# A weight unit is loaded between the first two attention chunks and converted earlier

## The chip, the cores and the metric

The kernel runs on one core of a Trainium2 chip. The time is the device time of one execution in microseconds (us). Engines: PE multiplies matrices, ACT and DVE work element by element, POOL does a few scalings, and the transfers of the part that matters here are issued by SP. Each engine works through its own queue of instructions in order, so an instruction that waits holds everything queued behind it on that engine.

## The reference

```python
scores = scale * np.matmul(q, k.transpose(0, 1, 3, 2))          # 4 batches, 8 heads, 576 positions, 64 wide
Dmat = np.where(rel >= 0, gamma ** rel, 0.0)                    # rel = row - column, one gamma per head
x = np.matmul(scores * Dmat, v)                                 # -> 2304 tokens x 512
h = x @ w_in;  g = np.where(h > 0, h, np.exp(np.minimum(h, 0)) - 1);  x = g @ w_out      # 512 -> 2048 -> 512
h = np.maximum(x @ w_in2, 0);  out = (h * h) @ w_out2
```

The four weight matrices come as 64-bit floats, q, k and v as well as the result are 32-bit.

## The kernel before

**Attention.** The decay mask is a product of a factor of the row and a factor of the column, so q and k are scaled by such factors and what is left is a causal mask. Tokens are taken in five blocks and each block in chunks of at most 128 positions. Block 0 is chunks 0 to 3 of batch 0; block 1 begins with the last 64 positions of batch 0 (chunk 4), then chunks 5 to 8 of batch 1, of which chunk 8 again has 64. A chunk has three pieces (`attn_pieces`). `transposes`: PE transposes the scaled q and k (L304) and ACT copies them out (L309). `scores`: PE multiplies them (L317), DVE masks the two halves (L320, tile P or spare). `values`: PE multiplies the state of the earlier chunks (L332, tile st) and the masked scores (L336) into ps_o, ACT and DVE split the result in a high and a low part (L161, L162, tile x), PE makes the chunk's own sum (L346, ps_u) and DVE adds it to the state (L352, or L354 where the state starts). q and k of chunks 0 to 3 are scaled by POOL, of the others by DVE (L278).

**Weights of layer 1.** A unit is 128 rows or columns of w_in or w_out, 512 KB as it lies in memory. `load_raw` (L198, L203) fetches it into a tile raw, `to_f32` turns the 64-bit floats into 32-bit ones (ACT L215 and L216; DVE L217, L218, L219, L222; tile f), `split_w` splits them (ACT L161, DVE L162; tile w). Units are taken in the order of use: unit 0 and 1 are w_in 0 and 1, unit 2 is w_out 0, then w_in 2, w_out 1, w_in 3 and so on. `w1_to(n)` converts up to n units; in it `w1_run` issues loads ahead (five units while `NURSERY` has places), then a split, then a conversion.

**Feed-forward of layer 1.** For a block and a w_in unit, `up` makes h with 12 matmuls (L174, L175, L176: high by high, high by low, low by high), ACT and DVE make g of it (L378, L379, L380; L382, L383; L161, L162), and `down`, two steps later, makes 12 matmuls into acc. h has two buffers, and the third `up` can start only when the first h has been read for the last time, by L383.

**What sets the order.** The source is recorded in program order, and a scheduler then places each engine's instructions by its own estimate of times. Loads marked `keep_in_program_order` stay as written; `tc.issue_after(i)` holds what is recorded inside it behind instruction i in the schedule. The head of the kernel is written by hand: the loads, then the pieces of chunks 0 to 3 in the order of `pieces`, with `EARLY` giving the units that are to be converted after each. 14 multiplications with zeros (`idle`, L171) are put between the last chunks. Later chunks are spread over the first steps of the feed-forward by `SPREAD`.

Layer 2 follows with a scheme of seven products in place of eight; the change does not touch it.

Of the kernel before, what the change touches and what calls it, by code (L numbers as in the profile page):

```python
# [127 lines left out]
def tile_kernel(ctx: ExitStack, tc, q, k, v, w_in1, w_out1, w_in2, w_out2, cst, out):  # L128
# [35 lines left out]
    def last_of(engine):  # L164
        return next(i for i in reversed(nc.cur_bb.bb.instructions) if i.engine == engine)

    def idle(n, ps, start=False):


        for _ in range(n):  # L170
            nc.tensor.matmul(ps, zero, ident.bitcast(BF16), start=start, stop=True, skip_group_check=True)  # L171
# [10 lines left out]
    def raw_place():  # L182


        n = at["raw"]
        if n >= NURSED:
            return raw_p.tile([P, DM, 2], I32, tag="raw", name="raw")
        if len(nursery) == n:
            tag, k = NURSERY[sum(n >= sum(m for _, m in NURSERY[:i + 1]) for i in range(len(NURSERY)))]
            t = wp.tile([P, k, DM, 2], I32, tag=tag, name="raw")  # L190
            nursery.extend(t[:, i] for i in range(k))
        return nursery[n]

    def load_raw(layer, which, f):
        w = ((w_in1, w_out1), (w_in2, w_out2))[layer][which].bitcast(I32)
        t = raw_place() if layer == 0 else raw_p.tile([P, DM, 2], I32, tag="raw", name="raw")
        if which == 0:
            i = nc.sync.dma_start(  # L198
                out=t.rearrange("p (k f) t -> p k (f t)", k=KC),
                in_=w[:, 2 * f * P:2 * (f + 1) * P].rearrange("(k p) f -> p k f", p=P),  # L200
            )
        else:
            i = nc.sync.dma_start(out=t.rearrange("p c t -> p (c t)"), in_=w[f * P:(f + 1) * P, :])  # L203
        if layer == 0:
            tc.keep_in_program_order(i)
        raws[layer, which, f] = t
# [47 lines left out]
    def load_chunk(ch):  # L254
        b, s, n = ch
        ts = []
        if ch in aside:

            t = wp.tile([P, 6, DM], F32, tag=f"w{9 - aside.index(ch)}", name="spare")
            spare[ch] = [t[:, i] for i in range(6)]  # L260
        for i, (src, nm) in enumerate(((q, "q"), (k, "k"), (v, "v"))):
            if ch in aside:
                t = spare[ch][i].rearrange("s (h d) -> s h d", h=H)
            else:
                t = n_p.tile([P, H, D], F32, tag=nm, name=nm)
            tc.keep_in_program_order(
                nc.sync.dma_start(out=t[:n], in_=src[b, :, s:s + n, :].rearrange("h s d -> s h d"))
            )
            ts.append(t)
        nat[ch] = ts  # L270

    def scale_chunk(ch):
        n = ch[2]
        qn, kn, _ = nat[ch]

        eng = nc.gpsimd if ch in blocks[0] else nc.vector
        for t, c in zip((qn, kn), scale_cols(ch[1])):
            eng.tensor_tensor(  # L278
                out=t[:n], in0=t[:n], in1=cs[:n, c:c + H].unsqueeze(2).to_broadcast([n, H, D]), op=ALU.mult
            )  # L280
# [439 lines left out]
    w1 = [(0, *u) for u in units]  # L720
# [12 lines left out]
    def load_next(late=False):  # L733
        if at["load"] < len(chunks) and (late or chunks[at["load"]][1] < 2 or chunks[at["load"] - 1][1] >= 2):
            load_chunk(chunks[at["load"]][0])
            at["load"] += 1

    def scale_next():
        if at["scale"] < at["load"]:
            scale_chunk(chunks[at["scale"]][0])  # L740
            at["scale"] += 1
# [15 lines left out]
    def step(name, limit, todo_, work):  # L757
        if at[name] < min(limit, len(todo_)):
            work(todo_[at[name]])
            at[name] += 1  # L760

    def w1_to(n):


        if at["split"] < min(int(n), len(w1)):
            with tc.issue_after(last_of(mybir.EngineType.Activation)):
                w1_run(n)

    def w1_run(n):
        while at["split"] < min(int(n), len(w1)):  # L770
            while at["raw"] < min(at["f32"] + (AHEAD_NURSED if at["raw"] < NURSED else AHEAD), len(w1)):
                step("raw", 99, w1, lambda u: load_raw(*u))
            step("split", at["f32"], w1, split_w)
            step("f32", at["raw"], w1, to_f32)
# [1 line left out]

    new_x(0)
    first = [attn_pieces(ch, 0) for ch in blocks[0]]
    load_next()
    load_next()  # L780
    for u in w1[:2]:
        load_raw(*u)
        at["raw"] += 1
    load_next()
# [3 lines left out]
    pieces = ((0, 0), (1, 0), (0, 1), (1, 1), (0, 2), (2, 0), (1, 2), (3, 0), (2, 1), (3, 1), (2, 2), (3, 2))  # L788
    for (c, piece), n in zip(pieces, EARLY):
        first[c][piece]()  # L790
        if (c, piece) == (3, 1):
            scored = last_of(mybir.EngineType.PE)
        if (c, piece) == (2, 2):
            rest = ps_h.tile([P, 512], F32, tag="h", name="rest")
            with tc.issue_after(scored):
                idle(14, rest[:, :256], True)
        w1_to(n)
        if piece == 0 and c < 2:
            scale_next()
        if (c, piece) in ((0, 2), (2, 0)):  # L800
            load_next()
    scale_next()
    at["next"] = len(first)
    pend = []
    seq = [(0, 0), (0, 1), (1, 0), (1, 1), (0, 2), (1, 2)] + [(f, c) for f in range(2, HF - 2) for c in range(NCH)]
# [130 lines left out]
```

## Time and profile before

| | us |
|---|---|
| median of 3 runs | 884.81 (883.24 to 886.2) |
| profiled execution | 884.94 |
| its span, first to last instruction | 883.0 |
| PE busy | 857.5 (97%) |
| DVE busy | 685.4 (78%) |
| ACT busy | 490.0 (55%) |
| granted PE clock, mean | 0.999 of full speed |

The profiled execution is 0.13 us above the median, and 1.94 us of it lie outside of the span. Busy times overlap; what PE does not fill of the span is 25.5 us. The profile names an idle time by what ended it: `[0.78 <-DVE P L320]` is 0.78 us of waiting that the DVE instruction of line 320, writing P, ended. Instructions of one engine overlap a little at their ends, so the distance between two starts is less than the duration in the row.

### The profile page before, as it was taken

The page shows a single profiled execution, that of the slowest core. Times are in us where ns is not written, and L with a number is a line of the kernel's source. Part 1 is how long each engine was busy: PE and PEld are TensorE (multiplying, and loading weights), DVE is VectorE, ACT ScalarE, POOL GpSimd, SP SyncE. Part 2 cuts the span into 40 slices and gives each one's busy share as a digit, 9 for nine tenths or more (in the row PEclk, how much of TensorE's full clock was granted, in tenths as well). Part 3 has the DMA queues.
Part 4 walks back from the last instruction along what each step waited for, and adds up shares of the span by engine and source line. Part 5 has one row for each costly group of instructions (what it writes and reads, how often), then busy time and mean ns, then how long its engine had stood idle before and what let it go on. Part 6 is the DMA issues. An engine that isn't in the chain of part 4 may idle for free.

```text
span 883.0 us, 15049 instructions
## 1 busy us (share of the span) xinstructions
PE 857.5 (97%) x5671; PEld 769.9 (87%) x5671; DVE 685.4 (78%) x1391; ACT 490.0 (55%) x961; POOL 9.6 (1%) x13
## 2 busy tenths in 40 slices
PE   7898999999999999999999999999999899999998
PEld 5686888888888888888888899999999889999997
DVE  4998978885668777766779866889883869899984
ACT  4764878664365565655757744556553434444441
POOL 4000000000000000000000000000000000000000
PEclk9999999999999999999999999999999999999999
DMA  9944306473539647434362053599979993444330
GB/s 222 289 105 159 120 16 176 144 202 96 131 88 248 151 149 215 132 120 155 128 229 74 24 161 122 181 321 340 337 239 362 402 336 126 162 143 145 121 131 36
DMA packets 157608, 155.33 MB, mean 176 GB/s; under 512 B 62816, under 2 KB 121312, under 8 KB 157536
## 3 DMA queue, kind: packets, MB, share of 16 engines
q1 hardware_dynamic: 150208, 139.69, 51.7%
q10 hardware_dynamic: 7328, 14.68, 4.5%
q8 instruction: 44, 0.72, 0.3%
q14 instruction: 28, 0.23, 0.1%
HBM read 98.77 MB, written 55.57 MB: 175 GB/s over the span
## 4 chain that ended last, share of the span: by engine, by line
PE 77%; DVE 10%; DMA 7%; ACT 2%; issue 2%; ACTq 1%; SPq 1%; POOL 0%; DVEq 0%
PE m L691 18%; PE A L505 8%; PE acc L174 7%; PE acc L175 7%; PE acc L176 7%; PE h L174 7%; PE h L176 6%; PE h L175 6%; PE D L505 4%; PE B L505 2%; DMA g2s<-go 2%; PE ps_o L336 1%; PE ps_s L317 1%; DVE go L532 1%; PE ps_t L304 1%
## 5 line engine op out<-in xcount | busy, mean ns | idle before, releaser
L691 PE MATMUL m<-wo,S 128*128 128x256 f32 x1512 | 183.4, 283 | 2.8 <-ACT S L161 2.4
L691 PEld LDWEIGHTS m<-wo,S 128*128 128x128 f32 x1512 | 182.0, 192 | 4.1 <-ACT S L161 3.3
L161 ACT CAST S<-g 128x512 fp32r<-128x512 f32 (+1 forms) x144 | 74.8, 565 | 96.1 <-DVE g L672 46.9
L174 PE MATMUL h<-x,w 128*128 128x512 f32 (+1 forms) x320 | 119.3, 374 | 4.6 <-DVE t L383 3.6
L175 PE MATMUL acc<-g,w 128*128 128x512 f32 (+1 forms) x320 | 118.6, 372 | 0.3 <-DVE g L162 0.3
L176 PE MATMUL h<-x,w 128*128 128x512 f32 (+1 forms) x320 | 118.2, 369 | 0.0
L175 PE MATMUL h<-x,w 128*128 128x512 f32 (+1 forms) x320 | 117.9, 369 | 0.2 <-DVE x L162 0.2
L176 PE MATMUL acc<-g,w 128*128 128x512 f32 (+1 forms) x320 | 117.5, 370 | 0.0
L505 PE MATMUL A<-T,pair 128*128 128x384 f32 x576 | 113.8, 336 | 2.8 <-DVE go L532 1.7
L174 PE MATMUL acc<-g,w 128*128 128x512 f32 (+1 forms) x320 | 110.9, 375 | 1.0 <-ACT w L161 0.8
L505 PEld LDWEIGHTS A<-T,pair 128*128 128x128 f32 x576 | 100.5, 188 | 5.4 <-DVE go L532 3.6
L162 DVE TENSOR_TENSOR S<-g,S 128x512 fp32r<-128x512 f32 (+1 forms) x144 | 85.5, 619 | 20.9 <-ACT S L161 19.3
L378 ACT ACTIVATE t<-h 128x512 f32<-128x512 f32 (+1 forms) x80 | 44.3, 554 | 80.7 <-PE h L176 76.7
L382 DVE SCALAR_TENSOR_TENSOR t<-e,t 128x512 f32<-128x512 f32 (+1 forms) x80 | 50.6, 633 | 45.4 <-ACT t L380 45.0
L174 PEld LDWEIGHTS h<-x,w 128*128 128x128 f32 x320 | 60.0, 188 | 16.7 <-DVE t L383 4.0
L161 ACT CAST g<-t 128x512 fp32r<-128x512 f32 (+1 forms) x80 | 46.1, 578 | 46.6 <-DVE t L383 46.2
L174 PEld LDWEIGHTS acc<-g,w 128*128 128x128 f32 x320 | 59.4, 188 | 12.0 <-ACT w L161 1.0
L175 PEld LDWEIGHTS acc<-g,w 128*128 128x128 f32 x320 | 60.3, 188 | 10.6 <-DVE g L162 0.5
L176 PEld LDWEIGHTS h<-x,w 128*128 128x128 f32 x320 | 60.2, 188 | 10.5 <-DVE w L162 0.2
L175 PEld LDWEIGHTS h<-x,w 128*128 128x128 f32 x320 | 60.2, 188 | 10.3 <-DVE x L162 0.5
L176 PEld LDWEIGHTS acc<-g,w 128*128 128x128 f32 x320 | 60.2, 188 | 10.2
L505 PE MATMUL D<-T,pair 128*128 128x384 f32 x288 | 58.1, 335 | 0.6 <-DVE T L162 0.6
(93 smaller groups left out, 1283.2 us busy)
## 6 DMA issues: line engine op xcount, KB each, us to landing
g2s<-go SPq DMA_DIRECT2D x48, 384.0 KB, 4.9
g<-g2s SPq DMA_DIRECT2D x36, 512.0 KB, 4.0
raw<-in_moe_w_in_dram SPq DMA_DIRECT2D x32, 512.0 KB, 5.8
raw<-in_moe_w_out_dram SPq DMA_DIRECT2D x32, 512.0 KB, 4.6
wo2s<-wo SPq DMA_DIRECT2D x56, 256.0 KB, 4.3
wo<-wo2s ACTq DMA_DIRECT2D x9, 1536.0 KB, 15.5
w2s<-f SPq DMA_DIRECT2D x32, 256.0 KB, 2.3
f<-w2s SPq DMA_DIRECT2D x32, 256.0 KB, 4.3
```

Source lines behind the costliest of these rows:

```text
L161: nc.scalar.copy(pair_hi, src)
L162: eng.tensor_tensor(out=pair_lo, in0=src, in1=pair_hi.bitcast(F32), op=ALU.subtract)
L174: nc.tensor.matmul(ps, l_hi, r_hi, start=first, stop=False)
L175: nc.tensor.matmul(ps, l_hi, r_lo, start=False, stop=False)
L176: nc.tensor.matmul(ps, l_lo, r_hi, start=False, stop=last)
L304: nc.tensor.transpose(ps[:, p, :n], t[:n, 2 * p:2 * p + 2, :].rearrange("s h d -> s (h d)"), ident[:n, :n])
L317: nc.tensor.matmul(ps[e][:n, p, :n], kT[r, p, :n], qT[r, p, :n], start=True, stop=True)
L336: nc.tensor.matmul(ps[e * D:(e + 1) * D, p, :n], vn[:n, 2 * p + e, :], live[e][:n, p, :n], start=not s, stop=True, skip_group_check=True,)
L378: nc.scalar.activation(t, h, AF.Relu, scale=-1.0)
L382: nc.vector.scalar_tensor_tensor(out=t, in0=e, scalar=1.0, in1=t, op0=ALU.add, op1=ALU.mult)
L505: ins = nc.tensor.matmul(ps, w[:, l, o:o + P], t[:, r, j], start=first and i + j == 0, stop=i + j == 3, skip_group_check=True)
L691: ins = nc.tensor.matmul(m(u, k), l[:, x], w[:, y], start=first and k in (1, 6, 4, 5), stop=j == HF - 1 and i == 2, skip_group_check=True,)
```

## The change

Three edits, all in the head of the kernel. The load of unit 0 is issued between the loads of chunk 0 and chunk 1; unit 1 stays between chunk 1 and chunk 2. The conversion of unit 0 is recorded after the transposes of chunk 0 and its split after the scores of chunk 0, each behind the last ACT instruction so far. The scaling of chunk 4 is held behind the state sums of chunk 2. Since unit 0 is then split before `w1_to(1)` is called, that call does nothing, and the four further loads that it used to issue come with the next call, after the loads of chunk 4.

```diff
     new_x(0)
     first = [attn_pieces(ch, 0) for ch in blocks[0]]
-    load_next()
-    load_next()
     for u in w1[:2]:
+        load_next()
         load_raw(*u)
         at["raw"] += 1
     load_next()
@@
         first[c][piece]()
+        if (c, piece) == (2, 2):
+            masked = last_of(mybir.EngineType.DVE)
         if (c, piece) == (3, 1):
             scored = last_of(mybir.EngineType.PE)
...
+        if piece < 2 and c == 0:
+            with tc.issue_after(last_of(mybir.EngineType.Activation)):
+                step(*(("split", 1, w1, split_w) if piece else ("f32", 1, w1, to_f32)))
         w1_to(n)
         if piece == 0 and c < 2:
             scale_next()
         if (c, piece) in ((0, 2), (2, 0)):
             load_next()
-    scale_next()
+    with tc.issue_after(masked):
+        scale_next()
```

The order of instructions changes with it on PE, DVE, ACT and SP up to about the sixth `up`; from there on it is the same but for a few neighbours that change places late in the kernel.

On DVE, at the very start, this stood before (P_184 and P_186 are the masked scores of chunk 0, f and raw tiles of the weight conversion, st the state):

```order
L320 TENSOR_TENSOR P_184<-ps_s,cs 128x512
L320 TENSOR_TENSOR P_186<-ps_s,cs 128x512
L354 COPY st<-ps_u 64x4x64 x2
L217 TENSOR_SCALAR f<-f 128x512
L162 TENSOR_TENSOR x<-ps_o,x 128x4x128
L218 TENSOR_SCALAR f<-f 128x512
L320 TENSOR_TENSOR spare<-ps_s,cs 128x512
L217 TENSOR_SCALAR f<-f 128x512
```

and this stands there now (P_191 and P_193 are the masks, w_195 the split weights):

```order
L217 TENSOR_SCALAR f<-f 128x512
L218 TENSOR_SCALAR f<-f 128x512
L320 TENSOR_TENSOR P_191<-ps_s,cs 128x512
L320 TENSOR_TENSOR P_193<-ps_s,cs 128x512
L219 SCALAR_TENSOR_TENSOR f<-raw,f 128x512
L222 ISA f<-raw,f 128x1024
L162 TENSOR_TENSOR x<-ps_o,x 128x4x128
L354 COPY st<-ps_u 64x4x64 x2
L162 TENSOR_TENSOR w_195<-f,w_195 128x512
L320 TENSOR_TENSOR spare<-ps_s,cs 128x512 x2
```

Two instructions of unit 0's conversion went ahead of the masks of chunk 0, and all of unit 0 ahead of the masks of chunk 1; unit 1's, of which the first stood between those masks, went behind them.

On PE, around the scores of chunk 2, this stood before (spare holds q, k, their transposes and masks of chunks 1 to 3; the first row is a transpose of chunk 2):

```order
L304 MATMUL ps_t<-cs,spare 128x128 x4
L336 MATMUL ps_o<-spare 64x128 x7
L304 MATMUL ps_t<-cs,spare 128x128 x4
L317 MATMUL ps_s<-spare 128x128 x8
L304 MATMUL ps_t<-cs,spare 128x128 x8
L332 MATMUL ps_o<-spare,st 128x128 x4
```

and this stands there now:

```order
L336 MATMUL ps_o<-spare 64x128 x8
L304 MATMUL ps_t<-cs,spare 128x128 x8
L317 MATMUL ps_s<-spare 128x128 x8
L304 MATMUL ps_t<-cs,spare 128x128 x4
L332 MATMUL ps_o<-spare,st 128x128 x4
```

The scores of chunk 2 (L317) stood behind the two transposes of chunk 2 alone; now the transpose of chunk 3's q stands between them.

On PE, in front of the third `up` (its weights are w_328; P_510 is a mask of chunk 4, and q and k of chunk 5), this stood before:

```order
L336 MATMUL ps_o<-P_510,v 64x64
L304 MATMUL ps_t<-cs,q 128x128 x4
L174 MATMUL h<-x,w_328 128x512
L175 MATMUL h<-x,w_328 128x512
L176 MATMUL h<-x,w_328 128x512
```

and this stands there now:

```order
L336 MATMUL ps_o<-P_510,v 64x64
L304 MATMUL ps_t<-cs,q 128x128 x4
L304 MATMUL ps_t<-cs,k 128x128 x4
L317 MATMUL ps_s<-qT,kT 128x128 x8
L174 MATMUL h<-x,w_328 128x512
```

The other transpose and the scores of chunk 5 went ahead of the third `up`. On DVE the instruction that frees a buffer of h for this `up` is the first L383. These rows led up to it before:

```order
L217 TENSOR_SCALAR f<-f 128x512
L320 TENSOR_TENSOR P_508<-ps_s,cs 64x4x64
L320 TENSOR_TENSOR P_510<-ps_s,cs 64x4x64
L278 TENSOR_TENSOR k<-k,cs 128x512
L222 ISA f<-raw,f 128x1024
L162 TENSOR_TENSOR w_328<-f,w_328 128x512
L218 TENSOR_SCALAR f<-f 128x512
L382 SCALAR_TENSOR_TENSOR t<-e,t 128x512
L162 TENSOR_TENSOR w_328<-f,w_328 128x512
L219 SCALAR_TENSOR_TENSOR f<-raw,f 128x512
L383 TENSOR_TENSOR t<-h,t 128x512
```

and these do now:

```order
L217 TENSOR_SCALAR f<-f 128x512
L222 ISA f<-raw,f 128x1024
L218 TENSOR_SCALAR f<-f 128x512
L217 TENSOR_SCALAR f<-f 128x512
L219 SCALAR_TENSOR_TENSOR f<-raw,f 128x512
L218 TENSOR_SCALAR f<-f 128x512
L382 SCALAR_TENSOR_TENSOR t<-e,t 128x512
L162 TENSOR_TENSOR w_328<-f,w_328 128x512
L222 ISA f<-raw,f 128x1024
L162 TENSOR_TENSOR x<-ps_o,x 128x4x64
L219 SCALAR_TENSOR_TENSOR f<-raw,f 128x512
L383 TENSOR_TENSOR t<-h,t 128x512
```

Between the state sums of chunk 3 (the last L352 before these rows) and the first L383 there were 13 DVE instructions; now there are 20, among them one more unit's conversion.

## Rows read from the trace of the kernel before

**Rows 1.** Busy time by stretch of the span; a stretch's length stands before the comma.
```profile
0.00:9.50 9.50, 6.79 (x31) 3.59 (x32) 0.48 (x1) 2.46 (x3) 3.54 (x8) 1.00 0.99 188
9.50:25.00 15.50, 11.91 (x138) 9.45 (x140) 13.27 (x22) 9.18 (x16) 6.08 (x5) 1.00 1.11 270
25.00:44.00 19.00, 16.25 (x179) 13.62 (x179) 17.65 (x35) 12.90 (x25) 0.00 (x0) 1.00 1.09 278
44.00:67.00 23.00, 23.00 (x142) 18.83 (x143) 22.86 (x43) 15.38 (x28) 0.00 (x0) 1.00 0.45 105
67.00:92.00 25.00, 22.30 (x231) 17.73 (x230) 19.65 (x37) 12.25 (x24) 0.00 (x0) 1.00 0.42 138
92.00:883.00 791.00, 777.20 (x4956) 706.68 (x4954) 611.54 (x1255) 437.79 (x868) 0.00 (x0) 1.00 0.55 175
```

**Rows 2.** PE in order of time: start, duration, what; idle before it.
```profile
12.67 1.16 PE L317 MATMUL ps_s<-spare 64*128 64x128 f32 x16
...
19.35 1.16 PE L317 MATMUL ps_s<-spare 64*128 64x128 f32 x16 [0.68 <-ACT spare L309]
21.18 0.65 PE L304 MATMUL ps_t<-cs,spare 128*128 128x128 f32 x4 [0.67 <-POOL spare L278]
...
30.70 1.13 PE L332 MATMUL ps_o<-spare,st 128*128 128x128 f32 x8 [1.40 <-DVE st L352]
...
43.90 0.47 PE L174 MATMUL h<-x,w 128*128 128x512 f32 x1 [1.13 <-DVE t L383]
...
46.75 0.60 PE L304 MATMUL ps_t<-cs,k 128*128 128x128 f32 x4
47.10 1.17 PE L174 MATMUL acc<-g,w 128*128 128x512 f32 x4
...
67.56 1.16 PE L317 MATMUL ps_s<-qT,kT 64*128 64x128 f32 x16
69.50 1.16 PE L332 MATMUL ps_o<-qT,st 128*128 128x128 f32 x8 [0.78 <-DVE P L320]
```

**Rows 3.** Busy time of one microsecond; the last number is GB/s.
```profile
11.00:12.00 1.00, 1.00 (x18) 0.83 (x17) 0.00 (x0) 0.59 (x1) 0.00 (x0) 1.00 1.10 349
```

**Rows 4.** ACT in order of time, and its group of L378.
```profile
12.10 0.67 ACT L215 ACTIVATE raw<-raw 128x512 int32<-128x512 uint32 x1 [0.23 <-DMA raw<-in_moe_w_in_dram]
...
38.28 0.60 ACT L378 ACTIVATE t<-h 128x512 f32<-128x512 f32 x1 [0.73 <-PE h L176]
...
L378 ACT ACTIVATE t<-h 128x512 f32<-128x512 f32 (+1 forms) x80 | 44.3, 554 | 80.7 <-PE h L176 76.7
```

**Rows 5.** POOL in order of time.
```profile
8.29 1.04 POOL L278 TENSOR_TENSOR spare<-spare,cs 128x512 f32<-128x512 f32 x1 [1.34 <-DMA spare<-in_q_dram]
9.50 1.04 POOL L278 TENSOR_TENSOR spare<-spare,cs 128x512 f32<-128x512 f32 x1 [0.16 <-DMA spare<-in_k_dram]
...
19.79 2.79 POOL L278 TENSOR_TENSOR spare<-spare,cs 128x512 f32<-128x512 f32 x2 [2.54 <-DMA spare<-in_q_dram]
```

**Rows 6.** DVE in order of time.
```profile
9.53 1.29 DVE L320 TENSOR_TENSOR P<-ps_s,cs 128x512 f32<-128x512 f32 x2 [8.13 <-PE ps_s L317]
...
21.60 1.52 DVE L162 TENSOR_TENSOR w<-f,w 128x512 fp32r<-128x512 f32 x1
...
24.24 0.68 DVE L162 TENSOR_TENSOR w<-f,w 128x512 fp32r<-128x512 f32 x1
...
35.32 0.85 DVE L352 TENSOR_TENSOR st<-ps_u,st 64x256 f32<-64x256 f32 x2
...
43.08 0.68 DVE L383 TENSOR_TENSOR t<-h,t 128x512 f32<-128x512 f32 x1
43.68 0.41 DVE L217 TENSOR_SCALAR f<-f 128x512 f32<-128x512 f32 x1
44.01 0.41 DVE L162 TENSOR_TENSOR x<-ps_o,x 128x256 fp32r<-128x256 f32 x1
...
68.75 1.29 DVE L320 TENSOR_TENSOR P<-ps_s,cs 128x512 f32<-128x512 f32 x2
```

## The prediction

> **What bounds the kernel now.** Read busy time by stretch first [rows 1]: PE fills 777.20 of the last 791 us and every one of the 23 us from 44 to 67. What it leaves is 2.71 us (9.50 less 6.79) up to 9.5, 3.59 up to 25, 2.75 up to 44, none up to 67, 2.70 up to 92 and 13.80 after. From 92 on the changed kernel has the same order on every engine but for a few neighbours, so I take those 13.80 us as kept: the change can give or take only in the first 92 us, where 11.75 us are idle on PE, and the first 2.71 of them lie ahead of everything that it moves. Then read who is full in the head: DVE works 13.27 of 15.50 us from 9.5 to 25, 17.65 of 19.00 up to 44 and 22.86 of 23.00 up to 67. So until about 44 DVE sets the pace, from 44 to 67 PE and DVE are both full, and from 67 to 92 they wait for each other. Last read PE's waits in order of time: 1.40 us for state sums at 30.70, 1.13 us for L383 in front of the third up at 43.90, 0.78 us for a mask at 69.50 [rows 2]. A gain must show there: the same PE work reached earlier.
>
> **The transfers.** Nothing is added: the bytes are the same. Unit 0 takes the place of chunk 1's q. Chunk 1's q and k were there just before 8.29 and 9.50, where POOL starts on them [rows 5]; 1.2 us lie between them, so the queue began on q at about 7.05. Unit 0, 0.524 MB at 349 GB/s [rows 3], takes 1.5 us: it lands at about 8.55, not shortly before 12.10, where ACT waited for it [rows 4]. Chunk 1 comes 1.5 us later (q 9.75, k 10.95). From unit 1 on the sum of bytes ahead is as before; chunk 4 now precedes units 2 to 5, which come some 1.7 us later and are not waited for, since unit 2's conversion stands behind the masks of chunk 2.
>
> **The head, step by step.** ACT's L215 and L216 end 1.3 us after 8.55 (0.67 each [rows 4]), at 9.9. L217 and L218 take 0.33 each (43.68 to 44.01 [rows 6]), so the masks of chunk 0, now queued behind them, run from 10.6 to 11.9. They ran from 9.53 to 10.82 [rows 6]: 1.1 us later. Chunk 1's k leaves POOL at 12.05 (1.04 each [rows 5]), its transposes stand behind the masked products of chunk 0 on PE (some 1.5 us from 11.9) and its scores start at about 14.6, not 12.67 [rows 2]: 1.9 later. DVE's two early L217 and L218 are thus paid for by the masks behind them.
>
> The next gate takes that delay up: chunk 2's scores, which started at 19.35, now stand behind the transposes of chunk 3's q, and these waited for POOL until 21.18 [rows 2, 5]. With 0.6 us for the transposes the scores start at about 21.75, 2.4 us later than before, whatever happened earlier. DVE has little to do meanwhile: unit 1's L217 stands ahead of those masks and behind chunk 1's x, and DVE is idle for some 0.8, 0.9 and 1.1 us in turn. One cost more: the split of a weight that ran beside POOL took 1.52 us, where the next took 0.68 [rows 6]; POOL was at work from 19.79 to 22.58 [rows 5]. Unit 1's L217 now falls there. The first bound is nothing, the other 1.0 us (POOL done at 22.6 where L217 would start at 21.6). I take 0.35, since POOL, not slowed by DVE in front, should end near 21.95.
>
> The Trainium skill, SBUF — State Buffer, section "SBUF: two separate sides", says that a DVE instruction of this kind and a POOL instruction exclude each other for their whole length, whichever came first; the 1.52 us row agrees. By it the masks of chunk 0 could lose some 1.7 us more beside chunk 1's scaling; the gate at 21.75 would take that up as well, so the sum would stay as it is, or be 0.65 higher with POOL's full 22.6.
>
> From the masks of chunk 2 (23.25) to the end of chunk 3's state sums I count on DVE 13 instructions of 0.6 us (the step from 43.08 to 43.68 [rows 6]), five of 0.33 and four state sums at half of 0.85: 11.15 us. Two waits come to it, unit 1's split for ACT's half of it (0.6) and chunk 3's masks for its scores (some 0.5), so 35.5, where before it was 36.17 (35.32 + 0.85 [rows 6]): the attention is 0.7 us ahead. It is no gain: an L218 and the split of unit 2, 0.93 us that DVE had done by then, now come after. At this point DVE is a quarter of a microsecond behind.
>
> **The third up is where time goes.** Between those sums and the first L383 DVE had 13 instructions, 6.9 us (36.17 to 43.08 [rows 6]). Now there are 20: twelve of 0.6, five of 0.33, two masks of half width (0.7) and an x of 0.34, 9.9 us. L383 then runs from 45.4 to 46.05, 2.3 us later. In front of the third up PE now also has the other transpose and the scores of chunk 5, and the scores wait for a copy that is the 16th ACT instruction from the first L378. That L378 began at 38.28 behind h [rows 4]; chunk 3's x, which h waits for, comes somewhat earlier, so I put it at 37.4, and 16 steps of 0.554 [rows 4] put the copy's end at 46.2. The scores run to 47.3, and the third up starts there and not at 43.90: 3.4 us later. Of these, the transposes (46.75 to 47.10, 0.35) and the scores (1.1 of the 1.16 of such a row) are work done ahead, 1.45 [rows 2]. PE is 1.95 us behind.
>
> **How much is given back.** From 43.90 PE ran without a gap up to 68.72, where it waited 0.78 us for the mask of chunk 6 until 69.50 [rows 2]. DVE is no more than 0.25 us behind at that mask: 2.3 later at L383, with 2.1 us more done. So the mask, at 68.75 before [rows 6], is there when PE comes at 68.72 + 1.95 = 70.67, and the 0.78 us are given back. 70.67 less 69.50 is +1.15 us. Behind it all waits up to 92 hang on chunk 6's result, in the same order, and move along. The third edit, the scaling of chunk 4 behind chunk 2's sums, costs two DVE steps that were there before, in nearly the same place; its cover is that nothing asks for chunk 4 until chunk 3 is through. If it were wrong by its whole length, it would be 1.2 us.
>
> **Sum.** 884.94 us (the span of 883.0 and 1.94 outside) + 1.15 = 886.1; the profiled execution is 0.13 above the median of 884.81, so 885.9 is forecast. What a measurement of this kernel can tell from no change is about 0.3%, 2.65 us: below 882.16 is faster, above 887.46 slower.
>
> **Rivals.**
> 1. *The lead is kept.* The 0.7 us that the attention is ahead reach the third up, the copy on ACT is not late, and PE has 1.45 us of work done ahead, so that it comes to the mask of chunk 6 up to 1.5 us earlier; since 2.1 us more of weight conversion is done by then, the 2.70 us of waits from 67 to 92 [rows 1] shrink too. For it: DVE, full from 25 on, has its order relieved by one unit. Against it: 20 instructions stand where 13 stood ahead of L383. It gives between 1.0 and 3.9 us: 881.0 to 883.9, in the middle 882.4.
> 2. *The clock falls at the third up.* From the end of the transposes, about 42, to 46.2 PE would have nothing to do for some 4 us. No gap since the start was longer than 1.40 us [rows 2], and the granted clock read 1.00 in every stretch [rows 1]. If it fell from the 2.4 GHz level to 1.2 for the third up alone, its 12 matmuls (43.90 to 46.75, 2.85 us [rows 2]) would take twice as long: 885.9 + 2.85 = 888.8, slower. It decides once the gap comes out near 4 us; at half of that the forecast holds. The Trainium skill, TensorE: Matmul & The Clock Gate, "HAM oscillation — how this bites in real kernels", tells of kernels whose bursts start at the low clock after such waits; no run here shows it yet.
> 3. *Nothing moves.* The raw unit lands early but DVE's total up to 67 is the same work, and both the late masks and the late L383 are taken up by gaps elsewhere: 884.8. For it: DVE's total is unchanged, and it sets the mask at 68.75.
>
> **How the numbers follow.** Forecast 0.50 (its own range 884.3 to 887.5, by the bounds 0 and 1.0 of the POOL cost and a microsecond on the ACT chain), rival 1 0.23, rival 2 0.14, rival 3 0.13. Faster: half of rival 1 (0.12) and 0.05 of the others together, 0.17. Slower: rival 2 but for 0.02 (0.12) and the upper end of the forecast (0.09), 0.21. The rest, 0.62, is no change. The range leaves out the low end of rival 1 and the far end of rival 2: 882.0 to 888.8.
>
> **What would show it.** In the profile after: unit 0's L215 near 8.6 and masks of chunk 0 behind 10.5; chunk 2's scores near 21.75 with a wait for POOL ahead; chunk 3's state sums ended before 36.17; the first L383 near 45.4 and the third up near 47 behind a PE gap of 3 to 4 us; no wait ahead of chunk 6's L332, at about 70.6. The prediction is wrong if the third up starts near 44 (rival 1), if a stretch around 47 shows a granted clock under 1.00 (rival 2), or if time moves behind 92, which I took as kept.

## The result and the profile after

| | before | after |
|---|---|---|
| median of 6 runs each, us | 885.06 (883.24 to 886.2) | 890.81 (886.91 to 894.63) |
| profiled execution, us | 884.94 | 886.91 |
| its span, us | 883.0 | 885.0 |
| its mean granted clock | 0.999 | 0.996 |

The ratio is 1.0067, with an interval of 1.0043 to 1.0091: slower by more than the 0.3% that can be told from no change, where 885.9 was forecast and 888.8 was the upper end of the range. The fall of rival 2 is what happened, but it is not the whole of the loss. The profiled execution is the fastest of the six; the others have a mean granted clock of 0.994 (three), 0.990 and 0.989.

The busy time by stretch of the changed kernel, with two stretches of 4 us behind (columns: stretch, its length, PE, PE weight load, DVE, ACT, POOL, granted clock, DMA share, GB/s; compare [rows 1]):

```profile
0.00:9.50 9.50, 7.36 (x26) 3.86 (x28) 0.48 (x1) 2.77 (x4) 2.50 (x7) 1.00 0.92 208
9.50:25.00 15.50, 11.14 (x136) 8.85 (x132) 11.26 (x20) 7.01 (x13) 6.94 (x6) 1.00 1.06 222
25.00:44.00 19.00, 17.61 (x186) 14.69 (x186) 18.02 (x37) 12.59 (x25) 0.00 (x0) 1.00 1.08 312
44.00:67.00 23.00, 20.86 (x119) 16.84 (x120) 22.83 (x43) 14.62 (x27) 0.00 (x0) 0.85 0.38 97
67.00:92.00 25.00, 23.24 (x205) 18.61 (x204) 18.74 (x34) 12.98 (x24) 0.00 (x0) 1.00 0.43 140
92.00:883.00 791.00, 780.86 (x5006) 710.24 (x5003) 614.63 (x1261) 440.40 (x872) 0.00 (x0) 1.00 0.54 174
44.00:48.00 4.00, 1.86 (x10) 1.46 (x12) 4.00 (x9) 4.00 (x9) 0.00 (x0) 0.60 0.98 255
48.00:52.00 4.00, 4.00 (x21) 3.25 (x18) 4.00 (x8) 1.52 (x3) 0.00 (x0) 0.55 0.09 19
```

Idle time of PE up to 92 is nearly what it was: 11.79 us against 11.75. What is new is the clock, 0.85 from 44 to 67, all of it between 44 and 52. A stretch's length times what its clock lacks is the clock time that it lost: 1.6 + 1.8 = 3.4 us.

PE of the changed kernel in order of time (start, duration, what; idle before it; compare [rows 2]):

```profile
8.75 1.16 PE L317 MATMUL ps_s<-qT,kT 64*128 64x128 f32 x16 [0.69 <-ACT kT L309]
11.71 0.66 PE L304 MATMUL ps_t<-cs,spare 128*128 128x128 f32 x4 [1.80 <-POOL spare L278]
...
15.89 1.16 PE L317 MATMUL ps_s<-spare 64*128 64x128 f32 x16 [0.42 <-ACT spare L309]
...
21.73 1.16 PE L317 MATMUL ps_s<-spare 64*128 64x128 f32 x16 [0.24 <-ACT spare L309]
...
42.66 0.66 PE L304 MATMUL ps_t<-cs,q 128*128 128x128 f32 x4
45.16 1.11 PE L304 MATMUL ps_t<-cs,k 128*128 128x128 f32 x4 [1.85 <-ACT qT L309]
47.25 2.08 PE L317 MATMUL ps_s<-qT,kT 64*128 64x128 f32 x16 [0.97 <-ACT kT L309]
49.26 0.79 PE L174 MATMUL h<-x,w 128*128 128x512 f32 x1
...
53.19 1.07 PE L174 MATMUL acc<-g,w 128*128 128x512 f32 x4
...
74.00 1.05 PE L332 MATMUL ps_o<-qT,st 128*128 128x128 f32 x8
```

Read the durations: chunk 1's scores took 1.16 us at 15.89, chunk 5's 1.8 times as long, 2.08 at 47.25. The transposes at 45.16 took 1.11 where those at 42.66 took 0.66. PE came out of a wait of 1.85 us at the 1.2 GHz level, worked for a microsecond, waited 0.97 more and went into the third up at that level. The up took 3.93 us (49.26 to 53.19) and not 2.85.

### The profile page after: what moved, and what is told of

It reads as the page before. It is cut to its first block, busy times and chain, and to the rows that moved or that the text cites. A ratio compares the mean times of both kernels' runs of the same rounds, so it can differ in the third digit from the quotient of the medians.

```text
span 885.0 us, 15044 instructions
## 1 busy us (share of the span) xinstructions
PE 861.1 (97%) x5671; PEld 773.1 (87%) x5671; DVE 686.0 (78%) x1391; ACT 490.4 (55%) x961; POOL 9.4 (1%) x13
## 4 chain that ended last, share of the span: by engine, by line
PE 83%; DVE 7%; DMA 4%; ACT 3%; issue 2%; ACTq 1%; SPq 1%; DVEq 0%
PE m L691 18%; PE A L505 11%; PE acc L174 7%; PE acc L175 7%; PE acc L176 7%; PE h L174 7%; PE h L176 6%; PE h L175 6%; PE D L505 5%; PE B L505 2%; PE ps_o L336 2%; PE ps_s L317 2%; DMA raw<-in_moe_w_in_dram 1%; PE ps_o L332 1%; PE ps_t L304 1%
## 5 line engine op out<-in xcount | busy, mean ns | idle before, releaser
L378 ACT ACTIVATE t<-h 128x512 f32<-128x512 f32 (+1 forms) x80 | 44.3, 554 | 80.2 <-PE h L176 76.1
L161 ACT CAST g<-t 128x512 fp32r<-128x512 f32 (+1 forms) x80 | 46.2, 579 | 48.0 <-DVE t L383 47.6
L176 PEld LDWEIGHTS h<-x,w 128*128 128x128 f32 x320 | 60.5, 189 | 10.6 <-DVE w L162 0.2
L162 DVE TENSOR_TENSOR g<-t,g 128x512 fp32r<-128x512 f32 (+1 forms) x80 | 50.5, 632 | 11.3 <-ACT g L161 11.0
```

The lines of the kernel that those rows point to most:

```text
L161: nc.scalar.copy(pair_hi, src)
L162: eng.tensor_tensor(out=pair_lo, in0=src, in1=pair_hi.bitcast(F32), op=ALU.subtract)
L176: nc.tensor.matmul(ps, l_lo, r_hi, start=False, stop=last)
L378: nc.scalar.activation(t, h, AF.Relu, scale=-1.0)
```

## The experiments

Theory A: the loss is granted clock, lost where PE now waits longer. Rival B: the new order itself is late (DVE or ACT chains, transfers), whatever the clock. Each kernel was timed beside the kernel before on the same chip. The table takes the two apart: the difference of the medians, the part of it that the difference in mean clock explains (0.885 us for each 0.001, a thousandth of the span; this is the highest price, as if all work stood still while clock is lost), and the rest. What each kernel is stands below the table.

| kernel | median (runs) | ratio, interval | over before | mean clock (before's) | by the clock | rest |
|---|---|---|---|---|---|---|
| after | 890.81 (6) | 1.0067, 1.0043 to 1.0091 | 5.75 | 0.9928 (0.998) | 4.6 | 1.1 |
| e8_after_again | 892.07 (5) | 1.0082, 1.0064 to 1.01 | 7.50 | 0.9914 (0.9989) | 6.6 | 0.9 |
| e7_head_fill | 891.59 (6) | 1.0073, 1.0057 to 1.0089 | 7.02 | 0.9928 (0.9989) | 5.4 | 1.6 |
| e11_head_more | 891.23 (7) | 1.0065, 1.0042 to 1.0087 | 6.10 | 0.9934 (0.9978) | 3.9 | 2.2 |
| e1_fill | 889.79 (12) | 1.0047, 1.0027 to 1.0067 | 4.38 | 0.9952 (0.9979) | 2.4 | 2.0 |
| e10_full_fill | 888.88 (12) | 1.0041, 1.0023 to 1.0059 | 3.75 | 0.9963 (0.9978) | 1.3 | 2.4 |
| e6_two_fills | 888.65 (5) | 1.0047, 1.003 to 1.0064 | 4.08 | 0.9970 (0.9989) | 1.7 | 2.4 |
| e2_loads | 888.54 (12) | 1.0027, 1.0008 to 1.0047 | 3.13 | 0.9961 (0.9979) | 1.6 | 1.5 |
| e3_steps | 886.69 (12) | 1.0004, 0.9985 to 1.0022 | 1.28 | 0.9977 (0.9979) | 0.2 | 1.1 |
| e5_norest | 886.56 (12) | 1.0, 0.9983 to 1.0017 | 1.15 | 0.9968 (0.9979) | 1.0 | 0.2 |
| e9_before_fill | 886.07 (12) | 1.0017, 1.0005 to 1.0029 | 1.50 | 0.9964 (0.9989) | 2.2 | -0.7 |

The clocks of the runs are told to 0.001 only, so a part may be off by some half a microsecond; for the first row that of before is the mean of its 70 runs beside the experiments. Over the 35 runs of before beside e1, e2, e3 and e5 the slope of time on clock was 0.70 us per 0.001, and 1.2 us of scatter stays that the clock does not explain. By that slope the part by the clock is four fifths of what stands in the table (3.7 for after), and the rest of the seven kernels with both halves of the change is 2.0 to 3.0 us.

**One half of the change at a time.** e2_loads issues only unit 0's load ahead of chunk 1, in the kernel before; e3_steps has the new order of conversions with the loads of before.

```diff
 # e2_loads, against before            # e3_steps is after with the reverse of this
-    load_next()
-    load_next()
     for u in w1[:2]:
+        load_next()
         load_raw(*u)
```

> The kernel before with the load of unit 0 ahead of chunk 1 and nothing else. The third up stands directly behind the first transpose of chunk 5, as before. Theory 1: no long PE gap, clock 0.998 or more, 884 to 887. Rival (delaying chunk 1's loads is what costs): 888 to 891 with a clock near 0.999.

> The changed kernel with both raw units loaded behind chunk 1 as before, so unit 0 lands near 12 us, but with the early conversion and split and the held scaling. The third up stands directly behind the first transpose of chunk 5. Theory 1: clock 0.998 or more, 883.5 to 886.5. Rival (recording the conversion early costs by itself, through the DVE order): 888 to 891.

The loads alone cost 0.27%, the steps alone nothing that can be measured; together they cost 0.67%. The time of e2_loads is in the range of its rival, but not at the rival's clock near 0.999; e3_steps is 0.2 us above the range of theory 1. In the profile of e2_loads, stretches of it lost clock too (columns as above), at waits of PE of 1.82 us ahead of chunk 2's scores and 1.53 us ahead of the third up:

```profile
24.00:28.00 4.00, 3.47 (x26) 2.95 (x22) 3.47 (x7) 2.33 (x5) 0.00 (x0) 0.59 1.11 326
48.00:52.00 4.00, 3.14 (x8) 2.50 (x9) 4.00 (x9) 2.97 (x6) 0.00 (x0) 0.57 0.96 263
```

The profile of e3_steps has falls too, 0.57 from 20 to 24 and 0.84 and 0.74 from 52 to 60, in an execution of 886.81 us.

**Zeros in the wait ahead of the third up.** e1_fill multiplies zeros there, 18 between the two transposes of chunk 5 and 10 ahead of its scores.

```diff
+                if ch == (1, 0, P):
+                    for many in ((9, 9) if nm == "qT" else (5, 5)):
+                        fill = ps_acc.tile([P, 512], F32, tag="acc", name="fill")
+                        with tc.issue_after(last_of(mybir.EngineType.PE)):
+                            idle(many, fill[:, :256], True)
```

> The changed kernel with 28 multiplications by zeros put on PE into its wait ahead of the third up: 18 between the two transposes of chunk 5 and 10 between the second and the scores, 0.12 us each; the order around is else the same up to the scores. Theory 1 (the PE clock falls in that wait, and how long it stays low makes the loss and the spread): mean granted clock 0.998 to 0.999 in every run, median 884 to 886, spread under 3 us. Theory 2 (the late third up itself costs the time, the clock is a symptom): the third up starts at 47 to 49 all the same and the median stays at 888 to 891.

The clock in its profile:

```profile
12.00:16.00 4.00, 2.59 (x21) 2.05 (x22) 3.69 (x6) 0.59 (x1) 1.03 (x2) 0.55 1.13 260
16.00:20.00 4.00, 3.73 (x34) 3.10 (x32) 2.04 (x4) 1.69 (x3) 2.68 (x3) 0.50 1.12 222
48.00:52.00 4.00, 3.67 (x35) 2.94 (x32) 4.00 (x8) 4.00 (x9) 0.00 (x0) 1.00 0.78 210
```

At the third up the clock stayed at the 2.4 GHz level. But this execution lost it in the head, between 12 and 24, a place where the profile of after had none. So there are two places. In this profile chunk 2's scores started at 26.43, 4.70 us later than in after, and the third up at 53.05. Theory 1 had the median wrong: 889.79 us lies in the range of theory 2.

**After once more** (the same kernel), to see whether the second place is its own.

> The changed kernel once more, for its clock in more runs and beside the others of this call. Theory 1 (its loss is the time that the PE clock stays low): median 889 to 891.5, time and mean granted clock go together at 0.7 to 1.0 us per 0.001, and the line through the runs gives 884.5 to 886 at a clock of 0.999. Rival (the new order costs the time): the line ends at 888 or more at 0.999.

Its profiled execution took 890.27 us, span 888.4; clock and PE of it:

```profile
12.00:16.00 4.00, 4.00 (x35) 3.41 (x35) 2.62 (x5) 1.17 (x2) 1.06 (x2) 0.50 1.20 265
16.00:20.00 4.00, 3.73 (x24) 2.99 (x24) 2.41 (x5) 1.10 (x2) 2.60 (x3) 0.50 1.13 217
48.00:52.00 4.00, 2.39 (x16) 2.00 (x18) 4.00 (x9) 3.65 (x8) 0.00 (x0) 0.59 0.86 230
52.00:56.00 4.00, 4.00 (x17) 3.10 (x16) 4.00 (x8) 1.45 (x3) 0.00 (x0) 0.56 0.01 1
```

```profile
11.72 1.12 PE L304 MATMUL ps_t<-cs,spare 128*128 128x128 f32 x4 [2.04 <-POOL spare L278]
...
17.53 2.08 PE L317 MATMUL ps_s<-spare 64*128 64x128 f32 x16 [0.27 <-ACT spare L309]
...
25.16 1.16 PE L317 MATMUL ps_s<-spare 64*128 64x128 f32 x16 [0.24 <-ACT spare L309]
...
52.67 0.79 PE L174 MATMUL h<-x,w 128*128 128x512 f32 x1
```

Both falls stand in one execution. The first follows the wait for POOL ahead of chunk 1's transposes, 2.04 us here and 1.80 in the other profile, where it had no fall; before, the longest wait there was 0.51. The four rows lose 7.4 us of clock time. Compare the two profiles of this one kernel: chunk 2's scores start 3.43 us later here (25.16 for 21.73), the third up 3.41 later, and the span ends 3.4 later. So the fall in the head costs time as well, and nothing behind it takes the delay up.

The line that the run was for did not come out. In its five runs the time does not go with the clock (890.27 us at 0.990, 892.07 at 0.995); through all eleven runs of the kernel the slope is 0.61 us per 0.001 and the value at 0.999 is 887.3, between theory 1 (up to 886) and the rival (from 888).

**Which of the two places costs.** e6_two_fills has 8 zeros in the head, recorded at chunk 1's transposes and executed ahead of chunk 0's scores, and 15 and 9 at the third up; e7_head_fill only the 8; e10_full_fill adds 6 behind chunk 0's scores to e6_two_fills; e11_head_more has the 8 and 6 alone. e7 and e11 keep the order of all else as in after.

```diff
+                if ch == (0, P, P) and nm == "qT":          # e6, e7, e10, e11
+                    with tc.issue_after(last_of(mybir.EngineType.PE)):
+                        idle(8, ps_h.tile([P, 512], F32, tag="h", name="fill")[:, :256], True)
...
+            if ch == (0, 0, P):                             # e10, e11, behind the scores
+                with tc.issue_after(last_of(mybir.EngineType.PE)):
+                    idle(6, ps_h.tile([P, 512], F32, tag="h", name="fill")[:, :256], True)
```

> The changed kernel with multiplications by zeros in its two long PE gaps: 8 (1 us) ahead of chunk 1's first transposes, 15 and 9 (1.8 and 1.1 us) around chunk 5's second transposes. Up to the third up its order is that of the changed kernel. Theory 1: mean clock 0.998 or more in most runs, median 884.5 to 887. Rival: 889 or more with the clock back at 0.998.

> The changed kernel with the 8 multiplications by zeros ahead of chunk 1's first transposes alone; every other instruction stands as in the changed kernel. If the wait ahead of the third up is the place where the clock falls: no change, 888.5 to 891.5 at a clock of 0.990 to 0.995. If the gap in the head weighs as much: half of the loss gone, 886.5 to 888.5 at 0.995 to 0.997.

> The changed kernel with 8 zero multiplications ahead of the scores of chunk 0 and 6 behind them, and 15 and 9 ahead of the third up. The order of all else is that of the version with fills at both places (888.65 us, which had 8 and none in the head). Theory A, the loss is low clock at the two places where PE waits longer than before: the six zeros cut the head's wait of 1.88 us ahead of the chunk 1 transposes to about 1.1 us (6 at 0.13 us each), the clock of 12 to 24 us stays at 1.00 in more of the runs, the mean clock is 0.998 or more, and the time is 886.0 to 888.0. Theory B, what is left of the loss at full clock is the order itself (PE 1.95 us behind at the third up, not given back): the clock may rise but the time stays at 888.0 to 889.0, some 0.4% above the kernel before.

> The changed kernel with the 8 and 6 zero multiplications in the head alone; the order of all else is exactly that of the changed kernel. Theory A: the head's low clock goes where it was, the one at the third up stays, so the mean clock is about 0.995 in nearly all runs and the time is 888.5 to 890.5, between the changed kernel's 890.8 to 892.1 and the version with both fills. Theory B, the head's low clock is hidden since POOL and DVE set the pace there: the time is that of the changed kernel, 890.8 to 892.1, as it was with 8 zeros (891.59).

Of the two places, zeros gave time back at the third up alone. The three kernels with zeros there come to 1.0041 to 1.0047 times the kernel before, the four without to 1.0065 to 1.0082. On one chip, e6 is 2.9 us below e7 and e10 2.4 below e11, with intervals that overlap. The profiles show it more sharply: from the start of chunk 2's scores to the end of the third up, where all else has the same order, after, e8, e7 and e11 took 31.46 to 31.92 us and e1, e6 and e10 29.48 to 29.51. The low clock there costs 2.0 to 2.4 us. e11_head_more, the head:

```profile
12.00:16.00 4.00, 2.41 (x35) 1.91 (x34) 3.49 (x6) 1.17 (x2) 0.83 (x2) 1.00 1.17 260
16.00:20.00 4.00, 3.58 (x46) 3.09 (x44) 3.72 (x6) 1.10 (x2) 2.70 (x3) 1.00 1.12 222
48.00:52.00 4.00, 3.84 (x20) 3.27 (x21) 4.00 (x8) 2.45 (x5) 0.00 (x0) 0.50 0.32 78
```

In this execution the head kept its clock (1.00 and 1.00), and the fall at the third up and the time of after remained. Part of that time is another wait, far behind:

```profile
273.87 0.39 PE L174 MATMUL acc<-g,w 128*128 128x256 f32 x1 [2.77 <-DVE x L421]
```

The same wait was 0.28 us in after and 1.85 in e1_fill; a fall followed it in e11 and e1. Its length differs between executions, and no run here looks into it. e10_full_fill, with the same zeros in the head as e11, read 0.79 from 12 to 16: whether the clock falls there differs between executions, and zeros did not settle it. They cut the wait for POOL to 0.59 and 0.71 us in these two, but one of 1.42 us for the masks of chunk 0 came behind it: DVE's L217 took 1.31 and 1.32 us beside POOL, and 0.43 in after. The third up in e6_two_fills:

```profile
22.54 1.16 PE L325 MATMUL ps_s<-spare 64*128 64x128 f32 x16 [0.24 <-ACT spare L312]
...
46.00 0.66 PE L307 MATMUL ps_t<-cs,k 128*128 128x128 f32 x4 [0.22 <-ACT qT L312]
46.49 1.15 PE L171 MATMUL fill<-cs,zero 128*128 128x256 bf16 x9
48.10 1.16 PE L325 MATMUL ps_s<-qT,kT 64*128 64x128 f32 x16 [0.46 <-ACT kT L312]
49.19 0.50 PE L174 MATMUL h<-x,w 128*128 128x512 f32 x1
...
52.05 1.07 PE L174 MATMUL acc<-g,w 128*128 128x512 f32 x4
```

Scores in 1.16 us and the up in 2.86 (49.19 to 52.05) again, and yet the third up starts at 49.19, as in after (49.26): chunk 2's scores were already 0.81 us later (22.54 for 21.73), in a head whose clock read 0.58 from 12 to 16. What is left of the loss of the three kernels at the clock of before, 2.0 to 2.4 us by the table, is put down to late order, B's part; it is a rest, and no run took it by itself. By their forecasts e6 lies between theory 1 (up to 887) and its rival (from 889), e7 at the upper end of no change, and e10 and e11 in the ranges of theory B; their mean clocks, 0.9963 and 0.9934, also stayed below what theory A asked for.

**The zeros of the kernel before.** It has 14 multiplications with zeros of its own between chunks 2 and 3. e5_norest has 1 in their place, e9_before_fill 24, and 8 more ahead of the third up.

```diff
-                idle(14, rest[:, :256], True)
+                idle(1, rest[:, :256], True)        # e5_norest; 24 in e9_before_fill
```

> The kernel before with one multiplication by zeros in place of 14 between chunks 2 and 3 (27.6 to 29.3 us): PE then has nothing for about 3 us there, and no instruction that the result needs moves. Theory 1 (a PE gap of 3 us or more can lower the clock whatever the kernel): a granted clock of 0.5 in some stretch after 30 us, mean clock 0.989 to 0.997, median 887 to 892, wide spread. Theory 2: as the kernel before, 884 to 886, clock 0.999.

> The kernel before with 24 in place of 14 multiplications by zeros between chunks 2 and 3 and 8 more ahead of the third up; all else stands as before. Theory 1 (the kernel before loses to a low clock too, in about half of its runs): clock 0.999 in nearly all runs, median 883.5 to 885, 0.5 to 1.5 us faster than the kernel before. Rival (zeros only delay the work behind them): 885.5 to 887.

Without them the time is the same within 0.17% either way, with a median between the two theories; its profile has the sign of theory 1, a clock of 0.51 and 0.50 from 32 to 40 around a wait of 2.58 us; four of its twelve runs had a clock of 1.000 and took 884.47 to 884.78, and four with 0.992 to 0.994 took 887.91 to 889.47. With more of them the kernel was 0.17% slower, as the rival had it and not theory 1. Its profile shows a wait ahead of chunk 2's values, and a clock of 0.58 from 24 to 28:

```profile
24.36 1.85 PE L337 MATMUL ps_o<-spare,st 128*128 128x128 f32 x8 [2.41 <-DVE spare L325]
```

One wait of 2.41 us stands here (2.42 in e5_norest) where the profile of before has three of 0.67, 0.80 and 0.49 us between 20.5 and 23.78, and no fall. A second stretch of low clock, 0.80 and 0.77 from 268 to 276, follows a wait of 1.90 us for DVE's x as in e11.

No version tried was faster than the kernel before.

## Why the prediction was wrong, step by step

**The step that failed** is that the clock was left out of the sum and put into a rival of chance 0.14, which was to decide "once the gap comes out near 4 us". The gap that was forecast, from 42 to 46.2, came, but it was never one of 4 us: PE waited 1.85 us, did the transposes, and waited 0.97 us; the clock fell all the same. In each of the four profiles of the order of after (after, e8, e7, e11) it fell at this place, in none of the three with zeros there (e1, e6, e10). The Trainium skill, TensorE: Matmul & The Clock Gate, "HAM oscillation — how this bites in real kernels", tells of a kernel whose bursts start at the low clock after each long wait for a transfer; the trace agrees that the burst starts low, with the scores at 2.08 us, here after the two waits of 1.85 and 0.97. The fall at the third up cost 2.0 to 2.4 us. A second step failed with it: a gate at chunk 2's scores was to take up the delays of the head, "whatever happened earlier". There is none (below), so a fall in the head goes through whole, 3.4 us in e8_after_again. On the medians the clock explains 3.7 of the 5.75 us by the slope of 0.70 and 4.6 at most, and 1.1 to 2.0 are left for the order. That this is near the +1.15 of the forecast is luck, as the next points show.

**The size of rival 2.** It priced the third up alone, at 2.85 us more. Measured on that up: 1.08 (3.93 less 2.85), since the clock came back in the middle of it; the scores ahead of it lost 0.92 as well, together 2.0. What the rival did not have is the other place, the head, with 4.0 us of clock time in the two rows of e8_after_again, and later falls: the profiles of e1 and e11 also read 0.66 to 0.67 from 276 to 280. The step that put chunk 1's scores at about 14.6 counted 1.9 us of delay and not the wait that PE has meanwhile.

**The transfers and the head.** ACT, DVE and POOL of the changed kernel:

```profile
9.08 0.67 ACT L215 ACTIVATE raw<-raw 128x512 int32<-128x512 uint32 x1 [0.39 <-DMA raw<-in_moe_w_in_dram]
...
38.40 0.62 ACT L161 CAST w<-f 128x512 fp32r<-128x512 f32 x1 [3.01 <-DVE f L222]
38.92 0.59 ACT L378 ACTIVATE t<-h 128x512 f32<-128x512 f32 x1
...
46.63 0.56 ACT L309 COPY kT<-ps_t 128x512 f32<-128x512 f32 x1
```

```profile
10.33 0.43 DVE L217 TENSOR_SCALAR f<-f 128x512 f32<-128x512 f32 x1 [8.93 <-ACT f L216]
10.79 1.15 DVE L218 TENSOR_SCALAR f<-f 128x512 int32<-128x512 int32 x1
11.86 1.27 DVE L320 TENSOR_TENSOR P<-ps_s,cs 128x512 f32<-128x512 f32 x2
...
22.84 0.43 DVE L217 TENSOR_SCALAR f<-f 128x512 f32<-128x512 f32 x1 [1.02 <-ACT f L216]
...
35.85 0.85 DVE L352 TENSOR_TENSOR st<-ps_u,st 64x256 f32<-64x256 f32 x2
...
46.83 0.68 DVE L383 TENSOR_TENSOR t<-h,t 128x512 f32<-128x512 f32 x1
```

```profile
10.33 2.51 POOL L278 TENSOR_TENSOR spare<-spare,cs 128x512 f32<-128x512 f32 x2 [2.98 <-DMA spare<-in_q_dram]
```

Unit 0 came half a microsecond later than forecast (9.08 for 8.55). The masks of chunk 0 ran from 11.86, not 10.6: beside POOL's scaling at 10.33, L218 took 1.15 us where 0.33 was counted. The Trainium skill, SBUF — State Buffer, "SBUF: two separate sides", has this as a lock that one of the two engines holds for its whole instruction, and the trace agrees. The masks themselves took 1.27 us for both, as before (1.29). Chunk 1's scores started at 15.89 (14.6 forecast), but chunk 2's at 21.73 (21.75). That the second figure fits is luck, since no gate took the delay up. From 15.89 on PE waited only 0.24 us, for ACT's copy and not for POOL, which began at 19.25, earlier than thought. In the five profiles of this order with the clock kept between the two (after, e6, e7, e10, e11) chunk 2's scores start 5.84 to 5.85 us behind chunk 1's, wherever these stand (15.89 to 18.32), and in the four without zeros ahead of it the third up starts 27.51 to 27.54 us behind chunk 2's scores. So every delay in the head arrives at the third up.

**Unit 1's conversion.** L217 started at 22.84, 0.9 us behind the 21.95 of the forecast, and not because of POOL, for which 0.35 us had been taken: POOL was done at 21.38, and L217 waited for ACT's L216, which ran from 22.14 to 22.80. From there the lead of 0.7 us at chunk 3's state sums was lost: they end at 36.70, for 35.5, half a microsecond behind the kernel before.

**The chain to the third up.** L383 ran at 46.83 (45.4), 1.4 late. The first L378 was at 38.92 (37.4). Its h was late: the first up waited 0.55 us for chunk 3's x and went on at 35.99, half a microsecond behind the kernel before (35.46), where the forecast had taken x to come earlier; h was there at 38.78. The split that stood ahead of L378 on ACT, after 3.01 us of waiting for DVE, cost it only the last 0.1. ACT then worked without a pause to the copy, which ended at 47.19 (46.2). So the third up began at 49.26 and not at 47.3: 1.0 us by the copy and 0.92 by the scores at the low level. That the copy, not L383, is the gate was right.

**What is given back.** "No wait ahead of chunk 6's L332" was right; it ran at 74.00, 4.50 us late for 1.15. Of the 3.35 us more, 3.0 are named: 1.0 for the copy, 0.92 and 1.08 for the clock; 0.35 are not. At the full clock it would still have been late by more than the forecast: from chunk 2's scores to this L332 the profiles with zeros took 50.34 to 50.38 us, before 50.15 and after 52.27, so with 2.38 us of delay at chunk 2's scores some 2.6 are the order's.

**The 13.80 us** taken as kept behind 92 were wrong, to the kernel's good: up to the end of its span at 885.0 its PE was idle for 12.14 (793 less 780.86). The same places late in the two kernels, before first:

```profile
536.02 1.33 PE L505 MATMUL A<-T,pair 128*128 128x384 f32 x6 [0.40 <-DVE go L532]
...
596.56 0.62 PE L505 MATMUL A<-T,pair 128*128 128x384 f32 x2 [0.44 <-DVE go L532]
...
655.77 0.97 PE L505 MATMUL A<-T,pair 128*128 128x384 f32 x4 [0.66 <-DVE pair L162]
...
686.91 1.32 PE L505 MATMUL A<-T,pair 128*128 128x384 f32 x6 [0.82 <-DVE go L532]
```

```profile
540.02 1.31 PE L505 MATMUL A<-T,pair 128*128 128x384 f32 x6 [0.37 <-DVE go L532]
...
658.31 0.97 PE L505 MATMUL A<-T,pair 128*128 128x384 f32 x4 [0.66 <-DVE pair L162]
```

PE was 4.50 us late at chunk 6, 4.00 at 536, 2.54 at 656 and 2.0 at the end of the span. The waits for `go` at 596 and 687, 1.26 us, are gone in the changed kernel: what they waited for was there when PE came. So of this execution the sum reads 4.50 late, less 2.5 given back, 2.0. The other executions lost more clock.

**What stays open.** Why one execution of a kernel loses the clock in the head and another not; the 1.2 us of scatter at one clock; why PE waits once for 2.4 us in e5 and e9 where the profile of before waits three times for less; and how much of the loss is the order's, which is known only as a rest.

## What to carry to other kernels

Price a new PE wait twice: its length, and the work behind it at half clock. Here 1.1 us of transposes between two waits did not keep the clock up; look at the waits around such a burst together, and at every place where an engine ahead of PE (here POOL, then ACT) was given more to do. Before a lead is counted, follow the queue of each engine in the chain for an instruction that waits for something else, as unit 1's L217 on DVE did for ACT (1.02 us). Before a later gate is trusted to take a delay up, look whether the engine really idles at it.

## What was not expected of the hardware

Two waits, of 1.83 to 1.85 and 0.97 to 1.45 us, with 0.66 to 1.11 us of transposes between, went with the 1.2 GHz level in all four profiles of that order. Of single waits in the head, one of 2.04 us was followed by it in one profile of after, one of 1.80 us in the other was not, and one of 1.62 to 1.64 us ahead of chunk 2's values was followed by it in none of seven. One and the same kernel ran at mean clocks from 0.989 to 0.996, worth 886.91 to 894.63 us; the kernel before, from 0.993 to 1.000, 882.69 to 890.37. Zeros at the third up kept the clock up where they cut the waits to 0.22 and 0.46 us, and left 3.75 to 4.38 us of a loss of 5.75 to 7.50.
